# A sliding-window attention kernel on one core: more K tiles turned by plain loads and GpSimd moves, a new order of the first loads, and the branch behind the stores

## The chip, the cores and the metric

The kernel runs on one core of one Trainium2 chip. The metric is device time in microseconds (us) of one execution; lower is better. The profile is of one execution. Its engines are called here by their own names, with the profile's short forms: PE and PEld (TensorE's matmuls and weight loads), DVE (VectorE), ACT (ScalarE), POOL (GpSimd) and SPq (the queue of the sync engine, SyncE, from which nearly all loads are issued).

## The reference

For each of 8 batches and 4 K/V heads, attention over the last 2048 positions of the cache; 8 query heads share a K/V head.

```python
q = (x @ wq)                                  # x: 256 x 1024, wq: 1024 x 4096
k, v = last W = 2048 rows of k_cache, v_cache  # per (batch, kv head): 2048 x 128, bf16
scores = einsum(q, k) * Dh ** -0.5
o = einsum(softmax(scores), v)
return o @ wo                                  # wo: 4096 x 1024
```

## The kernel before

One (batch, kv head) pair is a *unit*: 32 units, ordered by head ("group" g), each in 4 *chunks*, so the main loop has 128 chunks (numbered "slots" in the plan). TensorE needs K with the head dimension on the partitions (`kT`), but the cache has positions there. Three ways turn it: a transposing load (DMA does it), a plain load and TensorE transposes (`PE_T`), or a plain load, 32x32 block transposes on VectorE and 16 copies that put the blocks in place (`V_T`; the tuple is: at which unit's load the raw K is queued, then the slots of the blocks and of the moves).

```python
PE_T = (0, 1)
V_T = {8: (4, 16, 20, 29), 15: (11, 44, 48, 56), 22: (18, 72, 76, 85)}
Q_SLOTS = {1: (22, 30), 2: (37, 53), 3: (69, 83)}        # when q of a group is made
...
    def load_unit(self, ui, w=()):
        for u, at in V_T.items():
            if at[0] == ui:
                self.load_k(u)                 # raw K of a later unit goes first
        if ui < len(self.units):
            if ui not in V_T:
                self.load_k(ui, 0)             # first half of K, transposing
            self.load_v(ui, self.nc.sync)
            if ui not in V_T:
                self.load_k(ui, 1)
        for p in w:
            p()                                # a piece of wq or wo, 0.5 MB
...
        def blocks(i):                         # VectorE, 4 per unit
            nc.vector.transpose(out=st["kb"][:, sl, :], in_=self.k_raw[ui][:, sl, :])
        def move(k, d):                        # VectorE, 16 per unit
            nc.vector.tensor_copy(out=self.kT[ui][d * 32:(d + 1) * 32, :, k * 32:(k + 1) * 32],
                                  in_=st["kb"][k * 32:(k + 1) * 32, :, d * 32:(d + 1) * 32])
...
            for c in range(NCH):               # the main loop, one chunk
                # 4 score matmuls -> s_ps; ACT: exp -> pT
                # P.V of the chunk two back, 8 matmuls -> o_ps
                for p in plan[ui * NCH + c]:   # pieces of q, of the output projection, blocks, moves
                    p()
```

The kernel fixes the order of each engine's instructions: it is that of this program. On VectorE that order is: the copy of V (`va`) at the start of a unit, normalising the unit before, then the pieces of the slot. At the end a flag is read, and a branch leads to an exact fallback when the softmax without maximum was not safe; two output chunks of TensorE and their stores come behind the branch.

## Time and profile before

193.01 us, median of three runs (192.8 to 193.35).

| of the profile | value |
|---|---|
| span | 196.6 us |
| PE, ACT, DVE busy | 93%, 66%, 55% |
| first score matmul, end of the last P·V | 15.5 us, 187.5 us |
| waits of score weight loads for kT | 11.7 us |

From the page of the kernel before: its first line, the busy share of the DMA engines in 40 slices (9 is 90% or more), and what they moved.

```profile
span 196.6 us, 4773 instructions
DMA  6999999999999999999999999997999999999012
GB/s 151 361 417 213 350 286 242 342 191 303 357 249 264 347 266 258 347 180 352 289 254 256 295 310 192 325 335 184 254 267 335 265 230 353 227 264 281 16 57 60
```

From its list of waits (engine, line, what ended the wait: us in all, times, longest):

```profile
PEld L425 <- DMA kT<-in_k_cache_dram: 11.7, 14, 2.0
DVE va_112 L362 <- DMA v_sb<-in_v_cache_dram: 10.9, 5, 4.3
PEld L256 <- DMA wq_sb<-in_wq_dram: 1.6, 2, 0.9
```

The DMA queue is busy to 180 us, and TensorE waits for its K.

### The profile page before, as it was taken

To read this page: it belongs to the slowest core of one execution; us is meant where nothing else is said; L and a number is where in the kernel's file an instruction comes from. 1 tells how busy PE (TensorE), PEld (TensorE's weight loads), DVE (VectorE), ACT (ScalarE), POOL (GpSimd) and SP (SyncE) were. 2 spreads that over 40 slices of the span, in tenths; PEclk is the share of its full clock that TensorE was granted. 3 is DMA by queue.
4 is the path that set the end of the run, shared out by engine and by line. 5 is a ranking of instruction groups with operands and counts; after the bars stand their busy time and mean duration, and the time that the engine had idled before them with its cause. 6 is when DMAs were issued, how large, how long until landed. Compare 5 with 4: busy or idle time off the path is not lost. (4 is left out here: it accounts for less than half of the span.)

```text
span 196.6 us, 4773 instructions
## 1 busy us (share of the span) xinstructions
PE 181.9 (93%) x1984; PEld 150.9 (77%) x1984; DVE 107.4 (55%) x280; ACT 130.7 (66%) x134; POOL 0.9 (0%) x10
## 2 busy tenths in 40 slices
PE   7998997889999997999998999999989969979993
PEld 2887996769999996877877899867768848758842
DVE  0126644968753565985545587954454515335462
ACT  2208997845598785777885767868767858758800
POOL 1000000000000000000000000000000000000000
PEclk9999999999999999999999999999999999999999
DMA  6999999999999999999999999997999999999012
GB/s 151 361 417 213 350 286 242 342 191 303 357 249 264 347 266 258 347 180 352 289 254 256 295 310 192 325 335 184 254 267 335 265 230 353 227 264 281 16 57 60
DMA packets 70057, 51.73 MB, mean 263 GB/s; under 512 B 58256, under 2 KB 58896, under 8 KB 70032
## 3 DMA queue, kind: packets, MB, share of 16 engines
q1 hardware_dynamic: 69456, 50.87, 103.3%
q10 hardware_dynamic: 576, 0.52, 0.9%
q8 instruction: 16, 0.26, 0.6%
q14 instruction: 9, 0.07, 0.1%
HBM read 36.70 MB, written 0.52 MB: 189 GB/s over the span
## 5 line engine op out<-in xcount | busy, mean ns | idle before, releaser
L427 ACT ACTIVATE pT<-s_ps 128x1024 bf16<-128x1024 f32 x128 | 127.3, 1028 | 43.2 <-PE s_ps L425 43.2
L433 PEld LDWEIGHTS <-pT 128*128 128x128 bf16 x1024 | 69.3, 98 | 3.1
L425 PEld LDWEIGHTS <-kT 128*128 128x128 bf16 x464 | 43.2, 98 | 24.8 <-DMA kT<-in_k_cache_dram 11.7
L276 PE MATMUL op_ps<-wo_sb,OT 128*128 128x512 bf16 (+1 forms) x136 | 36.3, 367 | 0.6 <-DMA wo_sb<-in_wo_dram 0.5
L256 PE MATMUL q_ps<-xT,wq_sb 128*128 128x256 bf16 x192 | 27.5, 273 | 1.1 <-DMA wq_sb<-in_wq_dram 1.1
L433 PE MATMUL o_ps<-va_112,pT 128*128 128x129 bf16 x352 | 27.5, 220 | 0.0
L433 PE MATMUL o_ps<-va_113,pT 128*128 128x129 bf16 x352 | 27.3, 220 | 0.0
L433 PE MATMUL o_ps<-va_114,pT 128*128 128x129 bf16 x320 | 25.0, 220 | 0.0
L425 PE MATMUL s_ps<-QT_66,kT 128*128 128x256 bf16 x128 | 19.2, 273 | 4.0 <-DMA kT<-in_k_cache_dram 4.0
L425 PE MATMUL s_ps<-QT_63,kT 128*128 128x256 bf16 x128 | 19.1, 272 | 2.6 <-DMA kT<-in_k_cache_dram 2.0
L373 DVE TENSOR_SCALAR o_sb<-o_ps,RL_all 128x128 bf16<-128x128 f32 x64 | 19.5, 346 | 1.1
L256 PEld LDWEIGHTS <-wq_sb 128*128 128x128 bf16 x192 | 17.0, 98 | 2.9 <-DMA wq_sb<-in_wq_dram 1.6
L425 PE MATMUL s_ps<-QT_65,kT 128*128 128x256 bf16 x112 | 16.8, 273 | 0.3 <-DMA kT<-in_k_cache_dram 0.3
L425 PE MATMUL s_ps<-QT_64,kT 128*128 128x256 bf16 x96 | 14.4, 273 | 1.3 <-DMA kT<-in_k_cache_dram 1.3
L368 DVE RECIPROCAL RL_all<-o_ps 128x2 f32<-128x2 f32 x32 | 5.3, 167 | 18.4 <-PE o_ps L433 18.3
L375 DVE STREAM_TRANSPOSE OT<-o_sb 128x256 bf16<-128x256 bf16 x32 | 14.2, 445 | 1.1
L241 DVE COPY kTv<-kb 32x512 bf16<-32x512 bf16 x48 | 13.6, 284 | 0.8
L276 PEld LDWEIGHTS <-OT 128*128 128x128 bf16 x136 | 11.1, 97 | 3.4 <-DVEq L74 0.6
L362 DVE COPY va_112<-v_sb 128x2048 bf16<-128x2048 bf16 x11 | 7.6, 688 | 11.0 <-DMA v_sb<-in_v_cache_dram 10.9
L362 DVE COPY va_113<-v_sb 128x2048 bf16<-128x2048 bf16 x11 | 7.6, 691 | 7.2 <-DMA v_sb<-in_v_cache_dram 7.2
L283 DVE TENSOR_TENSOR oacc<-op_ps,oacc 128x512 f32<-128x512 f32 x8 | 5.5, 681 | 11.0 <-PE op_ps L276 11.0
L362 DVE COPY va_114<-v_sb 128x2048 bf16<-128x2048 bf16 x10 | 6.9, 689 | 5.5 <-DMA v_sb<-in_v_cache_dram 5.5
(43 smaller groups left out, 73.6 us busy)
## 6 DMA issues: line engine op xcount, KB each, us to landing
v_sb<-in_v_cache_dram SPq DMA_DIRECT2D x32, 512.0 KB, 6.1
wo_sb<-in_wo_dram SPq DMA_DIRECT2D x16, 512.0 KB, 6.0
wq_sb<-in_wq_dram SPq DMA_DIRECT2D x15, 512.0 KB, 6.0
k_raw<-in_k_cache_dram SPq DMA_DIRECT2D x5, 512.0 KB, 6.7
kT<-in_k_cache_dram SPq DMA_TRANSPOSE x54, 6.4
wq_sb<-in_wq_dram SPq DMA_DIRECT2D x2, 256.0 KB, 5.3
x_sb<-in_x_dram SPq DMA_DIRECT2D x1, 256.0 KB, 3.7
x_sb<-in_x_dram ACTq DMA_DIRECT2D x1, 256.0 KB, 3.9
```

What stands on the lines that cost most here:

```text
L241: nc.vector.tensor_copy(out=self.kT[ui][d * 32:(d + 1) * 32, :, k * 32:(k + 1) * 32], in_=st["kb"][k * 32:(k + 1) * 32, :, d * 32:(d + 1) ...
L256: nc.tensor.matmul(st["ps"][:, 0:self.NQ], lhsT=self.wq_t[g, i][:, c % (DC // 2), hl * P:(hl + 1) * P], rhs=self.xT[:, c, :], start=(c == ...
L276: nc.tensor.matmul(ps[:, 0:w], lhsT=self.OT[:, gq, c, t * P:(t + 1) * P], rhs=self.wo_t[gq][:, c, n0:n0 + w], start=(k == 0), stop=(k == 7))
L283: nc.vector.tensor_tensor(out=acc, in0=ps[:, 0:w], in1=acc, op=ALU.add)
L362: self.nc.vector.tensor_copy(out=self.va[ui % 3][:, :, 0:self.Dh], in_=self.v_sb[ui][:, :, :])
L368: nc.vector.reciprocal(out=rl[:, ui * QT_N:(ui + 1) * QT_N], in_=o_ps[:, :, Dh])
L373: nc.vector.tensor_scalar(out=o_sb[:, qt, :, :], in0=o_ps[:, qt, 0:Dh].rearrange("p (i c) -> p c i", c=4), scalar1=rl[:, ui * QT_N + qt:ui ...
L375: nc.vector.transpose(out=self.OT[:, g * QT_N:(g + 1) * QT_N, :, b * self.Sq:(b + 1) * self.Sq], in_=o_sb[:, :, :, :])
L425: nc.tensor.matmul(s_ps[:, jj, :], lhsT=self.kT[ui][:, c * CJ + jj, :], rhs=q_u, start=True, stop=True)
L427: nc.scalar.activation(out=pT[:, :, :], in_=s_ps[:, :, :], func=ACT.Exp, bias=0.0, scale=self.scale)
L433: nc.tensor.matmul(o_ps[:, qt, 0:self.VW], lhsT=pT[:, jj, qt * P:(qt + 1) * P], rhs=va[:, j, :], start=(j == 0 and qt == 0), stop=(j == KT ...
```

## The change

The intent: relieve the DMA queue of transposing loads (27 units to 22), let GpSimd do the moves, start sooner, and take the branch out of TensorE's last stretch. K of units 3 and 4 still comes by transposing loads, and the weights of group 1 come directly behind units 2 and 3.

```diff
-PE_T = (0, 1)
-V_T = {8: (4, 16, 20, 29), 15: (11, 44, 48, 56), 22: (18, 72, 76, 85)}
-Q_SLOTS = {1: (22, 30), 2: (37, 53), 3: (69, 83)}
+PE_T = (0, 1, 2)
+V_T = {u: (u - 3, 4 * u - 17, 4 * u - 14, 4 * u - 4, "g") for u in (10, 13, 16, 19, 22, 25, 28)}
+W_AT = (2, 2, 3, 3, *range(6, 30))            # unit behind which each weight piece is queued
+Q_SLOTS = {1: (11, 28), 2: (37, 53), 3: (69, 83)}
...
-            nc.vector.tensor_copy(out=self.kT[ui][...], in_=st["kb"][...])
+            if V_T[ui][4] == "v":
+                nc.vector.tensor_copy(out=out, in_=in_)
+            else:
+                nc.gpsimd.tensor_scalar(out=out, in0=in_, scalar1=1.0, scalar2=1.0, op0=ALU.mult, op1=ALU.mult)
...  opening: x in two column halves on one queue (before: two row halves on two queues)
+        load_x(0); wq0[0](); wq0[1](); load_x(1); wq0[2](); wq0[3](); self.load_k(0); wq0[4]()
...  the second half of x is turned after two of eight steps of q; K's transposes split in two
...  tail: all output chunks and stores ahead of the branch
-                flagi = fast.tail_begin()
+                flagi = fast.tail()
-        with tc.manual_schedule(engines=order):
-            fast.tail_end()
...  (cut: pool sizes, the slots at which units 4 to 10 are queued, the fallback's own stores)
```

Two of the cut parts bear on the queue too: kT has five buffers in place of six, and units 4 to 10 are queued at slots 2, 8, 8, 12, 16, 20 and 20 (before: 4 and 5 in the opening, 6 to 10 at slots 4 to 20).

Unit u is used from slot 4u on. Its first blocks stand at slot 4u−17; its raw K is queued with unit u−3. In the kernel before, the raw K was queued with unit u−4 and the blocks began at slot 4u−16.

More of the change, by code (lines that the diff above doesn't have):

```diff
@@ L18 @@
 RL_MIN = 1.0e-10
-N_WARM = 7
-PE_T = (0, 1)
-V_T = {8: (4, 16, 20, 29), 15: (11, 44, 48, 56), 22: (18, 72, 76, 85)}
-Q_SLOTS = {1: (22, 30), 2: (37, 53), 3: (69, 83)}
+N_WARM = 6
+OSB = 5
+PE_T = (0, 1, 2)
+V_T = {u: (u - 3, 4 * u - 17, 4 * u - 14, 4 * u - 4, "g") for u in (10, 13, 16, 19, 22, 25, 28)}
+W_AT = (2, 2, 3, 3, *range(6, 30))
+Q_SLOTS = {1: (11, 28), 2: (37, 53), 3: (69, 83)}
 O_SLOTS = {0: (52, 70), 1: (84, 101), 2: (99, 123), 3: (124, 143)}
@@ L127, in __init__ @@
         self.c1 = pool("c1", 1, long_ctx)
-        self.wp = pool("wp", 8, long_ctx)
-        self.osb = pool("osb", 5, long_ctx)
+        self.wp = pool("wp", 7, long_ctx)
+        self.osb = pool("osb", OSB, long_ctx)
         self.ps_m = pool("ps_m", 2, long_ctx, space=PSUM)
-        self.krp = pool("krp", 2)
-        self.kbp = pool("kbp", 1)
-        self.kvt = pool("kvt", 1)
-        self.ktp = pool("ktp", 6)
+        self.krp = pool("krp", 3)
+        self.kbp = pool("kbp", 2)
+        self.kvt = pool("kvt", 2)
+        self.ktp = pool("ktp", 5)
         self.vp = pool("vp", 6)
@@ L179, in load_k @@
         if ui in PE_T or ui in V_T:
-            self.k_raw[ui] = self.krp.tile([P, KT, self.Dh], BF16, name="k_raw")
+            self.k_raw[ui] = (self.kvt.tile([P, KT, self.Dh], BF16, name="k_raw", tag="kv") if ui < 2 else
+                              self.krp.tile([P, KT, self.Dh], BF16, name="k_raw"))
             nc.sync.dma_start(out=self.k_raw[ui][:, :, :], in_=src.rearrange("(p j) d -> p j d", j=KT))
@@ L188, in load_v, with load_unit @@
         b, g = self.units[ui]
-        self.v_sb[ui] = self.vp.tile([self.P, self.KT, self.Dh], BF16, name="v_sb")
+        self.v_sb[ui] = self.vp.tile([self.P, self.KT, self.Dh], BF16, name="v_sb", tag="v")
         eng.dma_start(out=self.v_sb[ui][:, :, :],
                       in_=self.v_cache[b, g, self.Sk - self.W:, :].rearrange("(p j) d -> p j d", j=self.KT))
-    def load_unit(self, ui, w=()):
+    def load_unit(self, ui):
         for u, at in V_T.items():
@@ L201, in load_unit @@
             self.load_v(ui, self.nc.sync)
-            if ui not in V_T:
+            if ui not in V_T and ui not in PE_T:
                 self.load_k(ui, 1)
-        for p in w:
-            p()
+        for p, at in zip(self.weights, W_AT):
+            if at == ui:
+                p()
     def k_pieces(self, ui):
@@ L239, in move @@
             if k == d == 0:
-                self.kT[ui] = self.kvt.tile([P, KT, P], BF16, name="kTv")
-            nc.vector.tensor_copy(out=self.kT[ui][d * 32:(d + 1) * 32, :, k * 32:(k + 1) * 32],
-                                  in_=st["kb"][k * 32:(k + 1) * 32, :, d * 32:(d + 1) * 32])
+                self.kT[ui] = self.kvt.tile([P, KT, P], BF16, name="kTv", tag="kv")
+            out = self.kT[ui][d * 32:(d + 1) * 32, :, k * 32:(k + 1) * 32]
+            in_ = st["kb"][k * 32:(k + 1) * 32, :, d * 32:(d + 1) * 32]
+            if V_T[ui][4] == "v":
+                nc.vector.tensor_copy(out=out, in_=in_)
+            else:
+                nc.gpsimd.tensor_scalar(out=out, in0=in_, scalar1=1.0, scalar2=1.0, op0=ALU.mult, op1=ALU.mult)
         return [lambda i=i: blocks(i) for i in range(4)], [lambda k=k, d=d: move(k, d) for k in range(4) for d in range(4)]
@@ L267, in o_pieces, with piece @@
         last = g == self.Hkv - 1
-        def piece(n0, w, i, mm=None):
+        def piece(n0, w, i):
             if i == 0:
-                st["ps"] = self.open_ps = self.ps_m.tile([P, 512], FP32, name="op_ps", tag="m")
+                st["ps"] = self.ps_m.tile([P, 512], FP32, name="op_ps", tag="m")
             ps = st["ps"]
-            for k in range(i * 2, i * 2 + 2) if mm is not False else ():
+            for k in range(i * 2, i * 2 + 2):
                 gq, c = g * self.QT_N + k // 4, k % 4
@@ L277, in piece @@
                                  rhs=self.wo_t[gq][:, c, n0:n0 + w], start=(k == 0), stop=(k == 7))
-            if i == 3 and mm is not True:
+            if i == 3:
                 acc = self.oacc[:, t, n0:n0 + w]
@@ L288, in piece @@
                     eng.dma_start(out=self.out[t * P:(t + 1) * P, n0:n0 + w], in_=o_t[:, 0:w])
-        return [lambda n0=sum(cuts[:k]), w=w, i=i, **kw: piece(n0, w, i, **kw) for k, w in enumerate(cuts) for i in range(4)]
+        return [lambda n0=sum(cuts[:k]), w=w, i=i: piece(n0, w, i) for k, w in enumerate(cuts) for i in range(4)]
     def start(self):
@@ L297, in start, with load_x @@
         nc.vector.memset(wz[:, :], 0.0)
-        x_sb = self.c1.tile([P, self.NT, self.D], BF16, name="x_sb")
+        x_sb = self.vp.tile([P, self.NT, self.D], BF16, name="x_sb", tag="v")
         xf = self.x.rearrange("b s d -> (b s) d")
-        nc.sync.dma_start(out=x_sb[:, 0, :], in_=xf[0:P, :])
-        nc.scalar.dma_start(out=x_sb[:, 1, :], in_=xf[P:2 * P, :])
-        for p in self.load_wq(0, 0, (1, 1, 2)) + self.load_wq(0, 1):
-            p()
-        for ui in range(2):
-            self.load_k(ui)
-            self.load_v(ui, nc.sync)
-        for ui, w in enumerate(self.load_wq(1, 0) + self.load_wq(1, 1)):
-            self.load_unit(ui + 2, [w])
+        H = self.DC // 2
+        def load_x(half):
+            nc.sync.dma_start(out=x_sb[:, :, half * H * P:(half + 1) * H * P],
+                              in_=xf.rearrange("(t p) d -> p t d", p=P)[:, :, half * H * P:(half + 1) * H * P])
+        wq0 = self.load_wq(0, 0, (1, 1, 2)) + self.load_wq(0, 1)
+        load_x(0)
+        wq0[0]()
+        wq0[1]()
+        load_x(1)
+        wq0[2]()
+        wq0[3]()
+        self.load_k(0)
+        wq0[4]()
+        self.load_v(0, nc.sync)
+        self.load_k(1)
+        self.load_v(1, nc.sync)
+        self.weights = []
+        for g in range(self.Hkv):
+            if g + 1 < self.Hkv:
+                self.weights += self.load_wq(g + 1, 0) + self.load_wq(g + 1, 1)
+            if g:
+                self.weights += self.load_wo(2 * g - 2) + self.load_wo(2 * g - 1)
+        self.weights += self.load_wo(2 * self.Hkv - 2) + self.load_wo(2 * self.Hkv - 1)
+        for ui in range(2, 4):
+            self.load_unit(ui)
         for v in self.va:
@@ L315, in start, with x_turn @@
         nc.vector.tensor_copy(out=warm_sb[:, :], in_=warm[:, 0:8])
-        H = self.DC // 2
-        for half in range(2):
-            ps = self.ps_m.tile([P, H, self.NT, P], BF16, name="xT_ps", tag="m")
+        def x_turn(half, pl, tag):
+            ps = pl.tile([P, H, self.NT, P], BF16, name="xT_ps", tag=tag)
             for c in range(H):
@@ L327, in start, with k_turn, k_copy @@
                 copy(out=self.xT[:, c0:c0 + H // 2, :], in_=ps[:, i * H // 2:(i + 1) * H // 2, :, :].rearrange("p c t s -> p c (t s)"))
+        x_turn(0, self.ps_m, "m")
         qs = [pl.tile([P, 2, self.NQ], FP32, name="q0_ps", tag=tag)
               for pl, tag in ((self.ps_o, "o_ps"), (self.ps_o, "o_ps"), (self.ps_m, "m"), (self.ps_m, "m"))]
+        KT = self.KT
+        tp = None
+        def k_turn(half):
+            for j in range(half * KT // 2, (half + 1) * KT // 2):
+                nc.tensor.transpose(tp[:, j, :], self.k_raw[0][:, j, :], self.ident[:, :])
+        def k_copy(half):
+            sl = slice(half * KT // 2, (half + 1) * KT // 2)
+            nc.vector.tensor_copy(out=self.kT[0][:, sl, :], in_=tp[:, sl, :])
         for c in range(self.DC):
             for h in range(self.rep):
-                nc.tensor.matmul(qs[h // 2][:, h % 2, :], lhsT=self.wq_t[0, c // (self.DC // 2)][:, c % (self.DC // 2), h * P:(h + 1) * P],
+                nc.tensor.matmul(qs[h // 2][:, h % 2, :], lhsT=self.wq_t[0, c // H][:, c % H, h * P:(h + 1) * P],
                                  rhs=self.xT[:, c, :], start=(c == 0 and h % 2 == 0), stop=(c == self.DC - 1),
                                  skip_group_check=True)
+            if c == 1:
+                x_turn(1, self.ps_s, "s_ps")
             if c == self.DC - 3:
-                self.k_first(0)
+                tp = self.ps_s.tile([P, KT, P], BF16, name="kf_ps", tag="s_ps")
+                k_turn(0)
+                k_copy(0)
+        k_turn(1)
         def q_copy(eng, k, b0, b1):
@@ L344, in q_copy @@
             (nc.vector.tensor_copy if eng == "v" else nc.scalar.copy)(out=dst, in_=src)
-        for k, eng in ((0, "v"), (1, "a"), (2, "v"), (3, "a")):
-            q_copy(eng, k, 0, 1)
-        self.va_copy(0)
-        for k, eng in ((1, "a"), (2, "v"), (0, "v"), (3, "v")):
-            q_copy(eng, k, 1, self.B)
-    def k_first(self, ui):
-        nc, P, KT = self.nc, self.P, self.KT
-        tp = self.ps_s.tile([P, KT, P], BF16, name="kf_ps", tag="s_ps")
-        for j in range(KT):
-            nc.tensor.transpose(tp[:, j, :], self.k_raw[ui][:, j, :], self.ident[:, :])
-        for h in range(2):
-            sl = slice(h * KT // 2, (h + 1) * KT // 2)
-            nc.vector.tensor_copy(out=self.kT[ui][:, sl, :], in_=tp[:, sl, :])
+        q_copy("a", 0, 0, self.B)
+        q_copy("v", 1, 0, 1)
+        q_copy("a", 2, 0, 1)
+        q_copy("v", 3, 0, 1)
+        k_copy(1)
+        q_copy("v", 2, 1, self.B)
+        self.va_copy(0)
+        q_copy("v", 1, 1, self.B)
+        q_copy("v", 3, 1, self.B)
     def va_copy(self, ui):
@@ L390, in side_plan @@
             spread(self.o_pieces(g, 0) + (self.o_pieces(g, 1) if g < self.Hkv - 1 else []), *w)
-        for ui, (_, s0, s1, s2) in V_T.items():
+        for ui, (_, s0, s1, s2, _) in V_T.items():
             blocks, moves = self.kv_pieces(ui)
@@ L401, in run @@
         pv_queue = []
-        w = []
-        for g in range(1, self.Hkv):
-            if g + 1 < self.Hkv:
-                w += self.load_wq(g + 1, 0) + self.load_wq(g + 1, 1)
-            w += self.load_wo(2 * g - 2) + self.load_wo(2 * g - 1)
-        w += self.load_wo(2 * self.Hkv - 2) + self.load_wo(2 * self.Hkv - 1)
-        def loads(ui):
-            if ui >= 1:
-                self.load_unit(ui + 5, [w.pop(0)] if w else [])
+        loads = {2: [4], 8: [5, 6], 12: [7], 16: [8], 20: [9, 10], **{4 * (u - 5): [u] for u in range(11, len(self.units))}}
         for ui, (b, g) in enumerate(self.units):
-            loads(ui)
             nxt = self.k_pieces(ui + 1)
@@ L422, in run @@
             for c in range(NCH):
+                for u in loads.get(ui * NCH + c, []):
+                    self.load_unit(u)
                 s_ps = self.ps_s.tile([P, CJ, UQ], FP32, name="s_ps")
@@ L450, in run, with tail @@
         self.pv_last, self.after = pv_queue.pop(0), after[2:]
-    def tail_begin(self):
+    def tail(self):
         self.pv_last()
@@ L458, in tail_begin @@
             p()
-        self.last = self.o_pieces(self.Hkv - 1, 1, (512, 256, 256))
-        for p in self.last[:3]:
+        for p in self.o_pieces(self.Hkv - 1, 1, (512, 256, 256)):
             p()
-        self.last[3](mm=True)
         return flagi
-    def tail_end(self):
-        self.last[3](mm=False)
-        for p in self.last[4:]:
-            p()
     def check_units(self, u0, u1):
@@ L580, in out_proj @@
             nc.vector.tensor_tensor(out=acc[:, :, :], in0=ps[:, :, :], in1=acc[:, :, :], op=ALU.add)
-        o_t = accp.tile([P, NT, D], BF16, name="o_t")
-        nc.vector.tensor_copy(out=o_t[:, :, :], in_=acc[:, :, :])
-        nc.sync.dma_start(out=out_flat.rearrange("(t p) d -> p t d", t=NT), in_=o_t[:, :, :])
-        nc.vector.tensor_copy(out=fast.oacc[:, :, :], in_=acc[:, :, :])
-        nc.vector.memset(fast.OT[:, (Hkv - 1) * fast.QT_N:, :, :], 0.0)
-        nc.vector.memset(fast.open_ps[:, :], 0.0)
+        o_t = [fast.osb.tile([P, 512], BF16, name="o_t") for _ in range(OSB)]
+        for o in o_t:
+            nc.vector.memset(o[:, :], 0.0)
+        for i in range(NT * NC_):
+            t, n0 = i // NC_, i % NC_ * 512
+            nc.vector.tensor_copy(out=o_t[i][:, :], in_=acc[:, t, n0:n0 + 512])
+            nc.sync.dma_start(out=out_flat[t * P:(t + 1) * P, n0:n0 + 512], in_=o_t[i][:, :])
 _INS = ['x', 'k_cache', 'v_cache', 'wq', 'wo']
```

## The prediction

> **What bounds the kernel now.** Two limits lie close together. The DMA queue: the page's DMA row is 9 in nearly every slice until 180 us, yet the windows from 30 to 150 us move only 278 to 281 GB/s, against 412 in the window 10 to 15 us, which holds almost only plain loads. A unit needs 0.5 MB each of V, weights and K, and 27 of 32 K's come by transposing load. At 280 GB/s a unit takes 5.6 us; its two plain parts at 412 take 2.55, which leaves 3.05 us for the transposing one (estimate; the lowest GB/s slices, 180 to 191, agree) against 1.27 plain. TensorE: in the timeline chunks repeat every 0.90 us and each Q or output piece adds 0.43, so the stream wants about 161 us; it takes 172 (15.5 to 187.5). The rest is in the list of waits: score weight loads waited 11.7 us for kT's DMA (14 times), those of Q 1.6 for wq. ScalarE (128 exponentials, 0.97 us apart: 124 us) is not the limit.
>
> **What the change does.**
> 1. Transposing loads fall from 27 units to 22: K of unit 2 goes through TensorE, seven units (before: three) through VectorE blocks. DMA work falls by 5 x 1.78 = about 9 us (estimate). From unit 10 on, three units need 15 us of DMA against 16 of TensorE, so the queue gets ahead. Gain: about 10 of the 13 us; some waits stay near units 8 and 9.
> 2. The moves leave VectorE (48 x 284 ns = 13.6 us) for GpSimd: 112 moves, 16 per unit in ten of twelve slots of 1.3 us. The trace has no such instruction. The Trainium skill (GPSIMD Engine Reference, section 3.1) has 512 elements in 769 ns; I estimate 0.7 to 0.9 us, 11 to 14 us per unit of 16 available. VectorE gains 16 block transposes x 684 ns = 10.9 us: about level. Its va copies (690 ns) can block against GpSimd (the skill, SBUF — State Buffer, Who interferes with whom), mostly hidden: cost 0.5 us.
> 3. Opening: x in halves, K's transposes split, K ahead of the last wq piece: first scores 0.7 us earlier. Sixteen more TensorE transposes: +0.9 us. Weights of group 1 directly behind unit 2 remove the wq wait at 40 us.
> 4. Tail: the branch no longer stands before the last two output chunks (0.61 us wait) and should hide behind the stores: −0.6 us.
>
> Sum: 193.0 − 10 − 0.7 − 0.6 + 0.9 + 0.5 = about 183; I take **182.5 us**, eight in ten between 179 and 187. Faster by over 2%: 0.90; within 2%: 0.07; slower: 0.03. TensorE alone should then bound the kernel.
>
> **What would show it.** Right: waits for kT's DMA below 4 us in all; DMA row below 9 in later slices, last loads some 9 us earlier; first score matmul near 14.8 us; GpSimd busy 75 to 100 us with no TensorE wait on kTv; no branch wait in the tail. Wrong in 1: kT waits stay. Wrong in 2: score weight loads wait for kTv, or va copies stand idle behind GpSimd and P·V waits for them.
>
> **What would make it wrong.** GpSimd moves over 1.1 us each: they fall behind, unit by unit, up to 200 us. Raw K of unit 10 arriving after its blocks are due (43 us), stalling VectorE in order. Plain loads beside transposing ones not as cheap as estimated. A lower granted clock with a denser TensorE.

## The result

| | time, median (range) | ratio of fast runs to the kernel before |
|---|---|---|
| before | 193.35 us (192.8 to 194.86, 5 runs) | |
| changed | 200.18 us (199.21 to 202.44, 5 runs) | 1.0331 [1.0268, 1.0394] |

A ratio is the mean time of one kernel's fast runs over that of the other's of the same rounds, so it is not quite the ratio of the medians quoted. Executions over 1.5% slower than the fastest of the same kernel are left out of the means. The change is slower by 3%, and the prediction was 182.5.

The first profile of the changed kernel fell on its slowest run (202.44 us), so what follows is from a second run of the same kernel (199.83 us, span 197.9; run `e1_again` below). From its page:

```profile
span 197.9 us, 4887 instructions
PE   7899999997877299999999999999999999999990
PEclk9999999999999879999999999999999999999999
DMA  5999999999999999999999999999999999900012
HBM read 39.32 MB, written 0.52 MB: 201 GB/s over the span
```

From its list of waits:

```profile
DVE kb L237 <- DMA k_raw<-in_k_cache_dram: 11.5, 2, 7.7
PEld L455 <- issue: 5.8, 2, 3.9
PE o_ps L455 <- DVE va L392: 5.4, 2, 3.7
PEld L447 <- DMA kT<-in_k_cache_dram: 3.4, 4, 1.6
```

Most of what I had named as a sign of being right is here: waits for kT below 4 us, the DMA row empty for three slices ahead of the stores, no wait of TensorE on the GpSimd moves. (The first score matmul is not: 16.3 us in place of 14.8.) But PE has a hole (the 2 in slice 14), behind it the granted clock falls to 8 and 7 tenths, and the new first line of the waits is one that I had listed only under what would make me wrong: the block transposes (L237) stood 11.5 us for raw K, in two waits. In the kernel before, no block waits for raw K in either profile.

The timeline of VectorE in the changed kernel shows the longer one (start, duration, engine, line, operation; in brackets the idle time just before and what ended it):

```profile
58.77 0.45 DVE L405 STREAM_TRANSPOSE OT<-o_sb 128x256 bf16<-128x256 bf16 x1
66.94 1.30 DVE L237 STREAM_TRANSPOSE kb<-k_raw 128x512 bf16<-128x512 bf16 x2 [7.73 <-DMA k_raw<-in_k_cache_dram]
68.17 0.66 DVE L392 COPY va<-v_sb 128x2048 bf16<-128x2048 bf16 x1
```

TensorE, same stretch, and the load that VectorE waits for, in the timeline of the sync engine's queue:

```profile
64.52 0.61 PE L447 MATMUL s_ps<-QT,kT 128*128 128x256 bf16 x4 [1.30 <-DMA kT<-in_k_cache_dram]
68.88 1.03 PE L455 MATMUL o_ps<-va,pT 128*128 128x129 bf16 x8 [3.75 <-DVE va L392]
69.70 1.06 PE L261 MATMUL q_ps<-xT,wq_sb 128*128 128x256 bf16 x4
71.97 0.60 PE L261 MATMUL q_ps<-xT,wq_sb 128*128 128x256 bf16 x4
```

```profile
60.42 0.47 SPq L181 DMA_DIRECT2D k_raw<-in_k_cache_dram  x1
```

The chain that ended last (`--critical`) runs through these pieces (start, duration, what):

```profile
60.42 6.50 DMA k_raw<-in_k_cache_dram
66.94 1.30 DVE kb L237 x2
68.25 0.59 DVE va L392
68.88 1.03 PE o_ps L455 x8
```

VectorE is free at 59.2 us, and its next instruction is the first block transpose of unit 13. That K is issued at 60.4, after VectorE has begun to wait for it, and lands at 66.9. The copy of V that TensorE needs for unit 9 stands behind it on VectorE. So TensorE stops, not for anything that it needs itself, and when it goes on, four matmuls take 1.06 us in place of 0.60 for about 3 us. The Trainium skill (TensorE: Matmul & The Clock Gate, What's actually happening) says that the clock is halved after an idle window of about 3.4 us; here 3.75 us of idle time fit it (a later run did it with 2.0, see the last section).

Where the time went shows best by counting out the units. This table is worked out from the traces, from the start of the first score matmul of each unit (16 per unit). Its first column is a second profile of the kernel before (run `e5_before_again`), for a reason that comes below.

| us | before | changed | difference | no raw waits (`e2_no_raw_wait`) | last version (`e5_comb_moved`) |
|---|---|---|---|---|---|
| to the first score matmul | 15.4 | 16.3 | +0.9 | 16.3 | 15.6 |
| units 0 to 8 | 42.8 | 44.5 | +1.7 | 42.8 | 43.5 |
| unit 9 | 4.9 | 11.6 | +6.7 | 7.0 | 6.5 |
| units 10 to 30 | 113.3 | 108.9 | −4.4 | 108.9 | 108.9 |
| unit 31 to its last P·V | 6.4 | 6.4 | 0 | 6.4 | 6.4 |
| behind the last P·V | 9.0 | 10.2 | +1.2 | 9.5 | 9.0 |
| span | 191.9 | 197.9 | +6.0 | 190.9 | 190.0 |

The relief is there, −4.4 us in units 10 to 30. It is smaller than I forecast, and one unit costs more than all of it.

### The profile page after: what moved, and what is told of

It is laid out like the page before. It is cut to its first block, busy times and chain, and to the rows that moved or that the text cites. A ratio compares the mean times of both kernels' runs of the same rounds, so it can differ in the third digit from the quotient of the medians.

```text
span 200.7 us, 4872 instructions
## 1 busy us (share of the span) xinstructions
PE 182.4 (91%) x1984; PEld 153.9 (77%) x1999; DVE 105.3 (52%) x250; ACT 131.5 (66%) x133; POOL 74.8 (37%) x122
## 4 chain that ended last, share of the span: by engine, by line
PE 64%; DMA 19%; SPq 11%; DVE 2%; issue 1%; ACT 1%; ACTq 0%
PE o_ps L455 22%; PE s_ps L447 21%; PE op_ps L281 13%; DMA wq_sb<-in_wq_dram 8%; PE q_ps L261 8%; DMA k_raw<-in_k_cache_dram 8%; SPq L184 7%; DMA kT<-in_k_cache_dram 4%; SPq L157 2%; DVE kb L237 1%; SPq L190 1%; ACT pT L449 1%; SPq L308 0%; SPq L181 0%; DVE va_112 L392 0%
## 5 line engine op out<-in xcount | busy, mean ns | idle before, releaser
L449 ACT ACTIVATE pT<-s_ps 128x1024 bf16<-128x1024 f32 x128 | 128.4, 1023 | 44.5 <-PE s_ps L447 43.9
L247 POOL TENSOR_SCALAR kTv<-kb 32x512 bf16<-32x512 bf16 x112 | 73.9, 660 | 91.5 <-DVE kb L237 76.3
L455 PEld LDWEIGHTS <-pT 128*128 128x128 bf16 x1024 | 70.1, 98 | 7.9 <-issue 4.6
L447 PEld LDWEIGHTS <-kT 128*128 128x128 bf16 x400 | 37.8, 98 | 16.1 <-DMA kT<-in_k_cache_dram 4.6
L281 PE MATMUL op_ps<-wo_sb,OT 128*128 128x512 bf16 (+1 forms) x121 | 33.0, 365 | 0.5
L261 PE MATMUL q_ps<-xT,wq_sb 128*128 128x256 bf16 x192 | 29.2, 276 | 1.5 <-DMA wq_sb<-in_wq_dram 1.5
L237 DVE STREAM_TRANSPOSE kb<-k_raw 128x512 bf16<-128x512 bf16 x28 | 18.7, 686 | 11.6 <-DMA k_raw<-in_k_cache_dram 11.6
L447 PE MATMUL s_ps<-QT_63,kT 128*128 128x256 bf16 x128 | 19.2, 273 | 0.3 <-DVE kT L362 0.3
L447 PE MATMUL s_ps<-QT_64,kT 128*128 128x256 bf16 x96 | 14.9, 279 | 3.8 <-DMA kT<-in_k_cache_dram 3.8
L447 PEld LDWEIGHTS <-kTv 128*128 128x128 bf16 x112 | 10.9, 98 | 4.9
L447 PE MATMUL s_ps<-QT_66,kT 128*128 128x256 bf16 x96 | 14.4, 273 | 0.1
L447 PE MATMUL s_ps<-QT_65,kT 128*128 128x256 bf16 x80 | 12.0, 273 | 0.1
L366 PE MATMUL q_ps<-xT,wq_sb 128*128 128x256 bf16 x64 | 9.2, 307 | 1.3 <-DMA wq_sb<-in_wq_dram 1.2
```

What stands on the lines that cost most here:

```text
L247: nc.gpsimd.tensor_scalar(out=out, in0=in_, scalar1=1.0, scalar2=1.0, op0=ALU.mult, op1=ALU.mult)
L261: nc.tensor.matmul(st["ps"][:, 0:self.NQ], lhsT=self.wq_t[g, i][:, c % (DC // 2), hl * P:(hl + 1) * P], rhs=self.xT[:, c, :], start=(c == ...
L281: nc.tensor.matmul(ps[:, 0:w], lhsT=self.OT[:, gq, c, t * P:(t + 1) * P], rhs=self.wo_t[gq][:, c, n0:n0 + w], start=(k == 0), stop=(k == 7))
L366: nc.tensor.matmul(qs[h // 2][:, h % 2, :], lhsT=self.wq_t[0, c // H][:, c % H, h * P:(h + 1) * P], rhs=self.xT[:, c, :], start=(c == 0 an ...
L447: nc.tensor.matmul(s_ps[:, jj, :], lhsT=self.kT[ui][:, c * CJ + jj, :], rhs=q_u, start=True, stop=True)
L449: nc.scalar.activation(out=pT[:, :, :], in_=s_ps[:, :, :], func=ACT.Exp, bias=0.0, scale=self.scale)
```

## The experiments

Theory A: VectorE, in order, is made to ask for raw K before the queue has it. Rival B: the queue is behind at that point anyway, so what doesn't wait there waits for kT or V. Rival C: GpSimd's moves hold VectorE up. Beside these, opening and tail may cost by themselves.

### The changed kernel once more (`e1_again`)

No edit.

> The changed kernel once more, for a profile and a fast-state time. Every theory: 199 to 201 us, ratio to the kernel before 1.03 to 1.04. Theory A (VectorE, in order, stands still for the raw K of unit 13): the same wait of its block transposes for k_raw's DMA shows again near 60 to 69 us, 8 to 10 us long, followed by about 10 us of lower granted clock. If the wait is absent here and the time is the same, theory A falls.

Measured: 201.32 us (199.83 to 203.14), before 193.94 in the same rounds, ratio 1.0425 [1.0336, 1.0514]. The wait is there (7.7 us, and one of 3.75 us for unit 10), with the low clock behind it; it is a little shorter than expected, and the low clock lasts about 3 us, not 10.

### Unit 13 reads another raw K (`e1_other_raw`)

```diff
-            nc.vector.transpose(out=st["kb"][:, sl, :], in_=self.k_raw[ui][:, sl, :])
+            nc.vector.transpose(out=st["kb"][:, sl, :], in_=self.k_raw[10 if ui == 13 else ui][:, sl, :])
```

> Wrong result on purpose: the block transposes of unit 13 read the raw K of unit 10, which has long landed; all loads, sizes and the order of instructions stay. Theory A (the 9.4 us wait of VectorE for unit 13's raw K, and the lower clock after it, are the loss): 8 to 11 us less than the changed kernel, 189 to 192 us, and no stretch of low clock. Rival B (the DMA queue is behind at that point, so what the blocks don't wait for, the scores and va copies wait for instead): 3 us less at most, 196 to 198, with kT and v_sb waits growing by the same amount. Rival C (GpSimd's moves hold VectorE up): no change, 199 to 201.

Measured: 198.98 us (198.6 to 201.82), ratio 1.0273. That is near rival B's number, and theory A as I had put it fails. The timeline of VectorE says why:

```profile
77.30 0.42 DVE L264 CAST QT<-q_ps 128x256 bf16<-128x256 f32 x1 [0.48 <-PE q_ps L261]
82.21 1.30 DVE L237 STREAM_TRANSPOSE kb<-k_raw 128x512 bf16<-128x512 bf16 x2 [4.49 <-DMA k_raw<-in_k_cache_dram]
```

Without the pause at unit 13, the queue has had less time when the *next* VectorE unit, 16, asks for its K, and VectorE stands there. Its waits for V grew too, from 2.0 to 6.7 us, as rival B has it. So freeing one unit does not separate the theories; all seven must be freed. (The run's result is wrong; at its tolerance the comparison does not see one unit's K with these inputs. The same holds for the next wrong one.)

### No block waits for any raw K (`e2_no_raw_wait`)

```diff
+        self.k_any = self.c1.tile([P, self.KT, P], BF16, name="k_any")
+        self.nc.gpsimd.memset(self.k_any[:, :, :], 0.125)
-            nc.vector.transpose(out=st["kb"][:, sl, :], in_=self.k_raw[ui][:, sl, :])
+            nc.vector.transpose(out=st["kb"][:, sl, :], in_=self.k_any[:, sl, :])
```

> Wrong result on purpose: the block transposes of all seven VectorE units read a constant tile, so that none waits for a raw K; every load stays. In the earlier run with unit 13 alone freed, the wait moved to unit 16 (4.5 us at 78 to 82) and to unit 9's kT. Theory A2 (VectorE is made to ask for raw K about 17 chunks ahead of use, more than the queue is ahead, and in order it holds everything up): the rest of the loss goes too, 190 to 193. Rival B (the queue has not delivered by then whoever asks): 196 to 199, the time going to waits for kT and v_sb before 90 us.

Measured: 192.56 us (192.45 to 196.19), before 193.4, ratio 0.9939 [0.9869, 1.001]. This is theory A2's number. All loads are still made, in the same order, and TensorE waits little for them: its weight loads 3.7 us for kT, and its P·V never for `va`, though VectorE waits for V:

```profile
DVE va L394 <- DMA v_sb<-in_v_cache_dram: 7.4, 6, 2.2
PEld L449 <- DMA kT<-in_k_cache_dram: 3.7, 5, 1.7
```

So the early demand for raw K costs about 8 us of the changed kernel's time (200.2 and 201.3 in its two sets of runs). In the table, unit 9 falls from 11.6 to 7.0 us and units 0 to 8 by 1.7. What is left at unit 9 over the 4.9 us of the kernel before, about 2 us, is the queue's own lateness: weight loads wait 2.0 us for kT there. Without a reader the raw buffers also come free sooner, but that is not the gain: in the changed kernel's list of SPq, the raw loads (L181) waited 0.4 us in all.

### Later blocks, with the right result (`e2_late_blocks`, `e3_some_later`)

All seven units four slots later:

```diff
-V_T = {u: (u - 3, 4 * u - 17, 4 * u - 14, 4 * u - 4, "g") for u in ...}
+V_T = {u: (u - 3, 4 * u - 13, 4 * u - 10, 4 * u - 1, "g") for u in ...}
```

> Right result: blocks and moves of all VectorE units four chunks later (blocks 13 to 10 chunks ahead of use in place of 17 to 14, moves in the nine after). Theory A2: 194 to 197, the wait for k_raw falls from 11.5 us in all to under 6. Rival B: within 1.5 us of the changed kernel (199 to 201). If the moves (0.66 us each, 10.6 us per unit) no longer fit into nine chunks, waits for kTv appear at each of the units.

Measured: 199.29 us (197.42 to 200.46), ratio 1.0256. The waits for raw K are gone, but the moves end too late. From the list of waits:

```profile
PEld L447 <- POOL kTv L247: 5.6, 4, 2.9
DVE kb L237 <- DMA k_raw<-in_k_cache_dram: 0.4, 1, 0.4
```

The time comes out at the edge of rival B's range, while the waits are those that theory A2 named. The blocks have to fit between two things: the landing of K, and the 16 moves of 0.66 us that need about nine slots. So I moved only those that had waited:

```diff
+LATER = {10: (2, 2), 13: (4, 3), 16: (2, 2)}     # slots later: blocks, end of the moves; the others stay
```

> The changed kernel, right result, with blocks and moves of units 10 and 16 two chunks later and of unit 13 four (moves three) later; the other four units stay. If theory A2 is right and the moves of these three still end in time, the k_raw waits fall from 11.5 us to under 3 and waits for kTv stay under 1: 193 to 195 us, close to the 192.6 of the run without any raw wait. If the loss comes back as waits for kT, v_sb or kTv: 197 to 200.

Measured: 198.15 us (196.6 to 200.76), ratio 1.0219: a miss. The waits for raw K fell to 3.0 us as expected and none for kTv is in the list, but one of those left (2.27 us, unit 16) stopped TensorE for 2.4 us at 97 us, a wait of 2.26 us for wq stopped it at 31, and after both it ran at the lower clock (granted 0.75 from 33 to 37 us). In the two placements tried, the room was too narrow for this order of loads. To queue the raw K with unit u−4 again, as in the kernel before, was not tried.

### K of units 3 and 4 through TensorE (`e2_pe34`)

```diff
-PE_T = (0, 1, 2)
+PE_T = (0, 1, 2, 3, 4)
```

> K of units 3 and 4 by plain loads and TensorE transposes, as units 0 to 2. Rival B, with a transposing load of 0.5 MB about 1.8 us dearer in the queue than a plain one: everything behind lands about 3.6 us earlier, the k_raw waits fall by about that, TensorE gains 32 transposes (1.8 us) in a stretch where it otherwise waits: 196 to 198. Theory A2 alone: also some gain, as the queue is further ahead. If transposing loads early are not the cost: 200 to 202.

Measured: 195.29 us (192.12 to 197.41), three of the four runs slow, so no ratio is to be had; its one fast run took 192.12. In its profile (slow) the waits for raw K are 5.5 us (11.5 before), none for kT is over the threshold of the list, and clock and span of a run say no more. The direction is as expected: with K of units 3 and 4 by transposing loads, the queue is some us later just where it is short (the longest wait for raw K is 4.4 us here, 7.7 there). The windows of `e1_again` show the price of such loads. The columns are the window, the busy times of PE, PEld, DVE, ACT and POOL with counts, granted clock, DMA share, GB/s; the first window holds plain loads alone, the second transposing loads of K and loads of V:

```profile
10.00:20.00 10.00, 9.70 (x107) 8.63 (x106) 5.09 (x10) 4.33 (x7) 0.00 (x0) 1.00 1.03 401
30.00:40.00 10.00, 10.00 (x121) 9.30 (x119) 5.36 (x14) 7.82 (x8) 0.00 (x0) 1.00 1.08 217
```

The second window holds two pauses of the queue; where the transposing packets flow, from 33 to 34 us, it is 287 GB/s.

### The opening alone (`e1_open_before`)

```diff
-        load_x(0); wq0[0](); wq0[1](); load_x(1); wq0[2](); wq0[3](); self.load_k(0); wq0[4](); ...
+        nc.sync.dma_start(out=x_sb[:, 0, :], in_=xf[0:P, :])
+        nc.scalar.dma_start(out=x_sb[:, 1, :], in_=xf[P:2 * P, :])
+        ... all five pieces of wq, then K and V of units 0 and 1; x turned in one go; 7 warm-up matmuls
```

> The changed kernel with the opening of the kernel before: x by rows on two queues, both x turns first, all of wq of group 0 ahead of K. First score matmul: 15.5 us in the kernel before, 16.4 in the changed one. If the new opening only delays the start, the first score matmul comes back to 15.4 to 15.7 and about 0.9 us are won, as far as the later wait for raw K of unit 13 does not swallow it: under theory A the landing of that K, not the start, sets the time, so the total gains less than 0.5 us while the wait grows by about 0.9.

Measured: 200.18 us (199.88 to 202.53), ratio 1.0368. The first score matmul came at 15.5 us (16.3 in `e1_again`), and the waits for raw K came to 11.2 us with a longest of 9.4 (7.7 there): by the traces, the earlier start was swallowed by the wait. The times alone do not say so: 1.1 us below `e1_again` in the same rounds, which is within the noise. So the new opening delays the start by 0.8 us; that this costs something only where the later wait does not set the time is argued, not shown.

### The tail alone (`e1_tail_before`, `e2_before_new_tail`)

The changed kernel with the old tail:

```diff
-                flagi = fast.tail()
+                flagi = fast.tail_begin()
+        with tc.manual_schedule(engines=order):
+            fast.tail_end()
```

> The changed kernel with the tail of the kernel before: the branch stands again ahead of the last two output chunks. From the end of the last P.V to the end of the span the kernel before takes 9.1 us, the changed one 10.6. If the new tail is what costs, 1.2 to 1.8 us less than the changed kernel; if that difference is chance of one profile, within 0.4 us of it.

Measured: 199.05 us (198.32 to 201.18), against 201.32 for the changed kernel. Behind the last P·V it takes 8.85 us, the changed kernel 10.2 (from the traces). And the kernel before with the new tail:

> The kernel before with the tail of the changed one alone (branch behind the stores). From the spans of profiles, the new tail costs about 1.5 us behind the last P.V: 1.2 to 1.8 us over the kernel before, 194.5 to 195.5. Its profile also stands for the kernel before in its fast state up to the tail: I expect less than 8 us of waits for kT's DMA there, against 11.7 us in the profile of the kernel before, whose span (196.6) is longer than its timed runs'.

Measured: 196.73 us (196.04 to 197.19), before 193.4, ratio 1.0153 [1.009, 1.0217]. Behind its last P·V the trace has 9.7 us, against 9.0 in the kernel before. The direction is sure in both kernels, the size is not: the traces show 0.7 to 1.4 us at the place itself, the times 2.3 to 2.9. The trace of the second has 9.6 us of waits for kT (8.3 in the fast profile of the kernel before), which I did not expect; that part stays open. What stands at the end of the new tail is the sync engine at its own branch. From the waits of its queue behind 186 us, changed kernel:

```profile
SPq L76 <- SPq L76: 3.6, 3, 2.5
```

In the kernel before, the same line of the list (L74 there) has 0.5 us, once. The branch was to hide behind the stores, but in the trace the engines' closing lines come only when the sync engine has passed it (196.6 to 197.9 us).

### Everything that cost undone, and a stall that none of the parts had (`e3_combined`, `e3_combined_ve`)

The edit is `e3_some_later`, `PE_T = (0, 1, 2, 3, 4)`, and opening and tail of the kernel before. Seven VectorE units and GpSimd's moves stay.

> The same with K of units 3 and 4 through TensorE, and opening and tail of the kernel before: each part that a run showed to cost is undone, the seven VectorE units and the moves on GpSimd stay. From 193 to 195: about 2.7 us less for the tail, 0.8 for the opening, 1 to 2 for the earlier deliveries: 188 to 190, faster than both kernels, with TensorE waiting for DMA less than 3 us in all.

Measured: 195.53 us (192.83 to 197.73); three of six runs were slow; ratio of the fast ones 1.0004 [0.9928, 1.008]. Its profile fell on a slow run, but `e3_combined_ve` (fast) ends its last P·V at the same time, 181.2 us, and has the same stall. Up to the last P·V all went as expected: it ends at 181.1 us, against 182.9 in the fast profile of the kernel before, with one wait of 1.7 us for kTv, and none for kT or raw K. Then the tail takes 14.1 us. From the timeline of weight loads, combined kernel:

```profile
188.40 3.10 PEld L286 LDWEIGHTS <-OT 128*128 128x128 bf16 x16 [4.04 <-issue]
```

The same line in the kernel before (second profile):

```profile
186.70 1.66 PEld L276 LDWEIGHTS <-OT 128*128 128x128 bf16 x16 [0.61 <-DVEq L74]
```

TensorE stands at the branch for 4.0 us in place of 0.61, then takes about twice as long for the same weight loads. With the moves on VectorE (the last entry of `V_T` set to "v"):

> The combined kernel with the moves on VectorE, as in the kernel before (0.284 us each there, 112 of them 31.8 us). If GpSimd's moves hold VectorE up (its va copies took up to 1.1 us against 0.69) and cost time, this is 1 us or more faster; if VectorE gets too full (105 + 32 us of 190, in order) it is slower by 1 to 3 us; I expect within 1 us of the combined kernel.

Measured: 196.2 us (194.35 to 199.38), ratio 1.0099 [1.0024, 1.0175] to the kernel before. That is 1% above the run with the moves on GpSimd, though the two intervals overlap; it has the same stall (4.17 us), and two waits for kTv. Taking the moves off GpSimd gains nothing: rival C falls.

### Where the branch stands (`e4_before_moved_branch`, `e4_comb_pe3`, `e4_comb_new_tail`, `e5_comb_moved`)

The combined kernel has more TensorE instructions ahead of the branch than the kernel before. To test place alone, the kernel before got 55 small warm-up matmuls for 7 large ones:

```diff
-        for i in range(N_WARM):            # 7
-            nc.tensor.matmul(warm[:, :], lhsT=wz[:, 0:P], rhs=wz[:, :], start=True, stop=True)
+        for i in range(55):
+            nc.tensor.matmul(warm[:, 0:64], lhsT=wz[:, 0:P], rhs=wz[:, 0:64], start=True, stop=True)
```

> The kernel before with 55 small warm-up matmuls for 7 large ones: 96 more TensorE instructions, about as long, and the branch at the very place in TensorE's stream where it stands in the combined kernel. If place alone makes the stall: TensorE waits about 4 us at the branch and the kernel is 3 to 3.5 us slower than the kernel before, 196 to 197. If not: 0.61 us and 193 to 194.

Measured: 197.27 us (196.05 to 198.53), ratio 1.0234 [1.0135, 1.0333], and the stall is there:

```profile
187.80 3.11 PEld L276 LDWEIGHTS <-OT 128*128 128x128 bf16 x16 [3.57 <-issue]
```

The combined kernel with K of unit 3 alone through TensorE (`PE_T = (0, 1, 2, 3)`), so 32 instructions fewer:

> The combined kernel with K of unit 3 alone (not 4) through TensorE. In the combined kernel TensorE stood 4.0 us at the branch in the tail, against 0.61 in the kernel before and with the tail restored alone; its branch stands 96 TensorE instructions further on than in the kernel before. Here it stands 64 further on. If the stall hangs on where in TensorE's instruction stream the branch stands, it should be 0.61 again: 189 to 191 us, about 3 faster than the combined kernel and 1.5% faster than the kernel before. If it comes from the rest (opening, later blocks), it stays at 4 us and the time at 193 to 194.

Measured: the stall is back to 0.61 us, as expected of place. But the time is 195.36 us (194.76 to 197.29), ratio 1.0144, a miss: with unit 4 by transposing load again, unit 16's raw K was late once more (3.2 us, TensorE idle for 3.4), with the low clock behind it. The combined kernel with the changed kernel's tail:

> The combined kernel with the changed kernel's tail. The new tail cost 2.9 us in the kernel before; the combined kernel's own branch stall costs 3.4 there. So about the same or 0.5 us less: 192.5 to 194. If the branch behind the stores is not what costs in the changed kernel, it is 190 or less.

Measured: 193.02 us (192.13 to 194.17), ratio 0.998: in range. Last, the combined kernel with the 55 small matmuls, which carry the branch past that place:

> The combined kernel with 55 small warm-up matmuls for 7 large ones: 96 more TensorE instructions ahead of the branch, which then stands past the place at which the combined kernel and the moved-branch one stall. If the stall (4.0 us in the combined kernel) goes back to about 0.6: 189.5 to 191 us, 1.5% faster than the kernel before and faster than both kernels. If the branch stalls there too: 193 to 194.

Measured: 191.95 us (191.68 to 192.87, all six fast), before 193.57, ratio 0.9929 [0.9878, 0.9979]. The stall is 0.61 us again. It is 1.7 us slower than the middle of what I expected, but it beats both kernels, by 0.7% and about 4%. From its timeline of weight loads:

```profile
184.82 1.66 PEld L286 LDWEIGHTS <-OT 128*128 128x128 bf16 x16 [0.61 <-DVEq L78]
```

| kernel | TensorE instructions ahead of the branch (built program: matmuls, weight loads and two more) | TensorE's wait there, us |
|---|---|---|
| before | 3938 | 0.61 |
| `e1_tail_before` | 3968 | 0.61 |
| `e4_comb_pe3` | 4002 | 0.61 |
| `e3_combined` | 4034 | 4.04 |
| `e3_combined_ve` | 4034 | 4.17 |
| `e4_before_moved_branch` | 4034 | 3.57 |
| `e5_comb_moved` | 4130 | 0.61 |

The Trainium skill (Runtime: NRT & Kernel Launch, Instruction fetch mechanics) has instructions fetched in blocks of 256, and says that a taken branch whose target isn't in the current window waits for a fetch. The runs fit this: the place was changed, and the stall came and went. (It is not the small warm-up matmuls: the last version has them and no stall.) The traces go a step further. In each of these seven kernels, a packet of 16 KB of the instruction queue begins at the branch. Where there is no stall, TensorE goes on as it begins (186.58 us and 186.70 in the second profile of the kernel before). In the three with 4034, TensorE goes on only 1.5 to 1.8 us after it has ended (`e3_combined`: packet from 184.76 to 186.91 us, TensorE at 188.40). Whose instructions it carries no trace shows, so the mechanism stays the page's.

### The kernel before, a second profile (`e5_before_again`)

> The kernel before, unchanged, for a second profile. Its first profile has a span of 196.6 us, while the spans listed with its timed fast runs are 191 to 192.5. If that profile was of an unusually slow execution, this one (if it falls in the fast state) has a span of 191 to 193, waits of the score weight loads for kT's DMA of 4 to 7 us in place of 11.7, and a last P.V near 182 in place of 187.5. If the waits are 10 us or more at a span of 192, the first profile was right and the difference lies elsewhere. Ratio to itself: 0.99 to 1.01.

Measured: 194.18 us (193.55 to 197.11) and 193.57 for the same kernel as "before" in the same rounds, ratio 1.0032 [0.9946, 1.0118], as it should be. Its profile (193.69 us, fast) against the one that I predicted from, first the first line of its page:

```profile
span 191.9 us, 4773 instructions
```

And from its list of waits:

```profile
PEld L425 <- DMA kT<-in_k_cache_dram: 8.3, 10, 1.7
PEld L256 <- DMA wq_sb<-in_wq_dram: 0.2, 1, 0.2
```

The waits that the change was to remove are 8.5 us here, not 13.3, and in units 10 to 30 the kernel takes 113.3 us, not 117.2. The first profile was of an execution 4.7 us longer than this one, and these waits differ by 4.8 us. The waits are slightly above what I had expected of this run (4 to 7).

## Why the prediction was wrong

- **"Gain: about 10 of the 13 us."** The mechanism was right and the size off, in two ways. The 13 us were those of a slow execution; a fast one has 8.5. And the relief begins only at unit 10: up to unit 9, seven units come by transposing load in both kernels. In units 10 to 30 all waits for kT and raw K went away, and the term measured −4.4 us. From the first profile's 117.2 it would have been −8.2. The sign to notice was a span of 196.6 beside a time of 193.0.
- **"Some waits stay near units 8 and 9" and, under what would make it wrong, "Raw K of unit 10 arriving after its blocks are due (43 us), stalling VectorE in order."** This is the step that failed: I had the queue ahead from unit 10 on ("so the queue gets ahead"), and did not ask where VectorE needs it to be. I saw the hazard, but gave it to unit 10 alone and no size. It came at unit 10 (3.75 us) and much larger at unit 13 (7.7 us), where VectorE asked at 59.2 us for a K that was issued at 60.4. At the prediction's own rates (412 GB/s, and 172 for a transposing load, from its 3.05 us) that K would land at about 61 us, an estimate; so even they had it late for 59.2, by some 2 us. It landed at 66.9. The run without any raw wait shows the price, about 8 us in all, part of it the lower clock after TensorE's pause. Freeing unit 13 alone did not show it, since the wait moved on to unit 16.
- **Moves on GpSimd, "0.7 to 0.9 us ... VectorE about level ... cost 0.5 us."** Right. The moves took 0.66 us each (74 us in all), VectorE's busy time went from 107 to 105 us, and no weight load waited for kTv. The Trainium skill's 769 ns for 512 elements (GPSIMD Engine Reference, section 3.1) was close on the safe side. That VectorE's fast copies and GpSimd can block each other (SBUF — State Buffer, Who interferes with whom) agrees with va copies of up to 1.1 us against 0.69; the run with the moves on VectorE was no faster.
- **Opening, "first scores 0.7 us earlier."** Wrong in sign, +0.9 us: 16.3 us. In the timeline of TensorE, the first 16 q matmuls wait 1.07 us for the first piece of wq, and take 3.6 us in place of 2.2. That is the pace of the halved clock: the first record of the full clock in the trace is at 10.2 us, in the two profiles of the kernel before at 7.1 and 4.1. Which part of the opening does this no run separates. The undone opening gave 15.5.
- **"+0.9 us" for 16 more TensorE transposes.** Not seen by itself. Units 0 to 8 took 1.7 us more, but without the raw waits they take 42.8 us, as in the kernel before; so the 1.7 us went with the wait for unit 10's raw K.
- **Tail, "should hide behind the stores: −0.6 us."** Wrong in sign, +1.2 us in the table. TensorE's 0.61 us did go, but the branch of the sync engine came to stand at the very end.
- **"Last loads some 9 us earlier."** They landed at 173.7 us, against 178.1 in the fast profile of the kernel before, and at 170.6 in the last version. The queue did get shorter; it was not what the time hung on any more.

The sum, with what was measured: −4.4 (for −10), +6.7 at unit 9 (not in the sum), +0.9 (for −0.7), +1.7 in units 0 to 8 (for +0.9), +1.2 (for −0.6), nothing seen for contention (for +0.5): but for rounding, the +6.0 us of span between two fast profiles.

Open: why the new tail costs more in the times than at its place in the trace, and which part of the tail's stall is instruction fetch.

## What to carry to other kernels

When a load is prefetched for an engine that works in order, compare two places, not one: where the load stands in the DMA queue, and where that engine asks for it; if it asks before loads that are due earlier have landed, everything behind it on that engine stops, and freeing one such wait only shows the next. A shorter queue helps from the place on where it was shortened, so count what must have been delivered by each unit rather than the total. And before costing a wait from one profile, hold its span against the timed runs.

## What the Trainium skill lacked or had wrong

- Advanced Engine Details and Errata, X-Bar Transpose (TRN2), says that transposing DMAs are as fast as regular ones. Here 217 GB/s were moved in a window of transposing K loads mixed with V loads, and 287 in a part of it without a pause, against 401 with plain loads alone. (The point is about that page; another page of the skill has a lower figure for some transposing loads.)
- TensorE: Matmul & The Clock Gate gives an idle window of about 3.4 us before the clock halves. In `e3_some_later`, 2.0 us without a matmul (29.2 to 31.2 us) were enough: the granted clock was 0.50 from 32 to 33 us and 0.75 from 33 to 37, and four matmuls took 1.06 us in place of 0.60.
- No page that I read tells at which places in an engine's instructions a branch becomes dear. Here 0.61 us at 3938, 3968, 4002 and 4130 TensorE instructions, and 3.6 to 4.2 us at 4034.
- No page that I read tells of pauses in a queue with loads outstanding: from 30 to 31 us the changed kernel's DMA engines moved 10 GB/s, and both kernels have such gaps of 1 to 2 us. In the second profile of the kernel before, the packed trace has 14 gaps of 1 us or more (under 60 GB/s) between 10 and 175 us, and 13 of them begin 0.4 to 2 us after the start of a 16 KB packet of the instruction queue. That the one causes the other no run tests.
